# Splitting step 11 of sixteen rounds as well, with the cast of that step on ScalarE

## The chip, the cores and the metric

The kernel runs on one core of one Trainium2 chip. The metric is the device time of one execution in microseconds, as the median of repeated runs; less is better. The chip's engines have short names in what follows: PE is TensorE (matmuls), PEld its weight loads, DVE is VectorE, ACT is ScalarE, POOL is GpSimd, SP is SyncE, which issues the DMAs. Each engine works through its own instructions in the order in which they were written, and waits on semaphores for those of other engines.

## The reference, cut to what matters

The program computes an agent attention over two batches of 12480 tokens with 128 channels and 49 agents, and then a two-layer network with an ELU between the layers:

```python
a2k = sm(agents, k); agent_v = a2k @ v          # softmax over the 12480 keys
q2a = sm(q, agents); x = q2a @ agent_v          # softmax over the 49 agents
h = x @ w_in                                    # 128 -> 2048
g = np.where(h > 0.0, h, np.exp(np.minimum(h, 0.0)) - 1.0)
out = g @ w_out                                 # 2048 -> 128
```

All of it is in float32.

## The kernel before

The tokens are cut into 26 groups of 960, called rounds (13 per batch). The product `agent_v @ w_in` is folded into one small matrix per batch, so that a round needs only the 49 softmax weights of each token. A round has 16 steps: two halves of 480 token columns on each of two row groups, times eight chunks `c` of 256 hidden units. Step `s` is round `s // 16`, and its number in the round is `s % 16`; chunk `c` is `s % 8`. Step 11 of a round is thus chunk 3 of the second half.

One step is a chain across engines:

- `p1(s)` (L406): six matmuls (L413) make `h` for 256 hidden units and 960 tokens in a PSUM buffer of two banks. There are three such buffers, taken in turn by `slot()` (L151). The same three serve the attention work.
- `elu(s)` (L415): ACT computes `e = relu(-h)` (L419) and `e = exp(-e)` (L422), DVE computes `g = max(e - 1, h)` (L424), after which the PSUM buffer is free.
- `split(s)` (L426): in the steps for which `is_split(s)` holds, DVE rounds `g` to `hi` in the format float32r (L431), and POOL computes the remainders `lo = g - hi` as two instructions (L204, a helper). There are three buffers for `hi` and three for each `lo`.
- `p2(s)` (L436), which runs four steps later (`LAG = 4`) behind `p1(s + 4)`: the second layer (L453), added up in PSUM over the eight chunks. Where the step is split it is 12 matmuls in float32r: `w_lo * hi`, `w_hi * hi` and `w_hi * lo`, over two halves of the chunk and two row groups. Where it is not split it is 4 matmuls in float32, each of which the trace shows as two.

`SPLITS` lists the chunks that are split: 1, 3, 4, 6, 7 in general, and 1, 4, 6, 7 in the second half of a round that is "covered". A round is covered when there is a visit at its step 11. A visit (L629) is a piece of attention work that takes one of the three PSUM buffers at the end of a step: scores of later queries (`q`), scores of the second batch's keys (`k`), or products with its values (`e`). Visits at step 11 are in rounds 0 to 10 and in rounds 12, 14, 16, 18, 20 and 22; in rounds 1 to 8 there is another one at step 1. In steps 4 and 12 that are not covered, `p1` of the next step is issued one step early.

The order on each engine is written out by hand: the loop at the end (L722 on) issues, for each step, `p1`, `p2` of four steps earlier, `elu`, `split`, and then the attention work planned for that step. To a visit at step 11 belong an exponential of 392 columns on ACT (`q_exp`, L307) behind `split` of step 12, reductions on DVE at steps 12 to 14, and in rounds 4 to 7 also subtractions on DVE (`e_sub`, L208) and exponentials on ACT (`e_exp`, L211) at steps 13 and 14. In the last step of each half the partial sums leave PSUM: ACT copies `oa` (L468) between the two activations of steps 3 and 11, and POOL adds (L469).

The lines that decide what is split:

```python
SPLITS = ((1, 3, 4, 6, 7), (1, 4, 6, 7))                                   # L49
return c in SPLITS[half if j * NM + NP + LAG in covered else 0]            # L403
```

Of the kernel before, what the change touches and what calls it, by code (L numbers as in the profile page):

```python
# [13 lines left out]
ALU = mybir.AluOpType  # L14
# [10 lines left out]
def tile_agent_attention_moe(  # L25
# [10 lines left out]
    nc = tc.nc  # L36
# [5 lines left out]
    NM = DFF // 128  # L42
# [5 lines left out]
    LAG = 4  # L48
    WARM = 2  # L49
    LEAD = 6  # L50
    NP = NM // 2
    EDGE = (NP - 1 + LAG) % NP
    SPLITS = ((1, 3, 4, 6, 7), (1, 4, 6, 7))
# [143 lines left out]
    def cast_hi(eng, out, x):  # L197
        if eng is nc.scalar:
            nc.scalar.activation(out=out, in_=x, func=ACTF.Copy)
        else:  # L200
            eng.tensor_scalar(out=out, in0=x, scalar1=1.0, scalar2=0.0, op0=ALU.mult, op1=ALU.add)

    def rest(eng, out, x, hi):
        eng.tensor_tensor(out=out, in0=x, in1=hi.bitcast(F32), op=ALU.subtract)  # L204
# [179 lines left out]
    def wo_hi(c):  # L384
        for x in (2 * c, 2 * c + 1):
            if x in SPLIT:
                cast_hi(nc.scalar, w_part(w_hi, x), w_e[x])
# [6 lines left out]
    h_t, e_t, g_t, hi_t, lo_t, o_t = {}, {}, {}, {}, {}, {}  # L394

    def at_step(s):

        x, c = divmod(s, NP)
        return x // 2, x % 2, c

    def is_split(s):
        j, half, c = at_step(s)
        return c in SPLITS[half if j * NM + NP + LAG in covered else 0]  # L403

    def p1(s):
        j, half, c = at_step(s)  # L406
        h = slot()
        ah, al = A[j // NG, c]
        hi, lo = p_t[j]
        for i, (a, p) in enumerate([(ah, hi), (ah, lo), (al, hi)]):  # L410
            for u, r in enumerate(ROWS):
                x = slice(r, r + NA)
                nc.tensor.matmul(out=h[:, u, 0:T], lhsT=a[x, :], rhs=p[u ^ half][x, :], start=i == 0, stop=i == 2)  # L413
        h_t[s] = h[:, :, 0:T]

    def elu(s, between=None):

        h, e = h_t.pop(s), x_p.tile([128, 2, T], F32, tag="e", name="e")
        nc.scalar.activation(out=e, in_=h, func=ACTF.Relu, scale=-1.0)  # L419
        if between:  # L420
            between()
        nc.scalar.activation(out=e, in_=e, func=ACTF.Exp, scale=-1.0)  # L422
        g = g_p.tile([128, 2, T], F32, tag="g", name="g", bufs=5)
        nc.vector.scalar_tensor_tensor(out=g, in0=e, scalar=-1.0, in1=h, op0=ALU.add, op1=ALU.max)  # L424
        g_t[s] = g

    def split(s):
        if not is_split(s):
            return
        hi_t[s] = g_p.tile([128, 2, T], F32R, tag="hi", name="hi", bufs=3)  # L430
        nc.vector.tensor_copy(out=hi_t[s], in_=g_t[s])  # L431
        lo_t[s] = []
        for i in range(2):
            lo_t[s].append(g_p.tile([128, T], F32R, tag=f"lo{i}", name=f"lo{i}", bufs=3))
            rest(nc.vector if s == S - 1 else nc.gpsimd, lo_t[s][i], g_t[s][:, i, :], hi_t[s][:, i, :])

    def p2(s):
# [6 lines left out]
        if is_split(s):  # L444
            x, hi, lo = SPLIT.index(c), hi_t.pop(s), lo_t.pop(s)
            jobs = [(w[:, x, i], hi[:, i, :]) for w in (w_lo, w_hi) for i in range(2)]
            jobs += [(w_hi[:, x, i], lo[i]) for i in range(2)]
        else:
            jobs = [(w_f[:, PLAIN.index(c), i], g[:, i, :]) for i in range(2)]
# [28 lines left out]
    def at(s, fn, *a):  # L478
        pre.setdefault(s, []).append((fn, a))

    with tc.manual_schedule():
        with tc.tile_pool(name="pro", bufs=6) as pro:
# [128 lines left out]
            def A_part(c, eng):  # L611
                A_pe(0, 512 * c, 512 * c + 512, banks[c])
                A_out(0, 512 * c, 512 * c + 512, eng)
# [9 lines left out]
        groups[0] = 32  # L623
        mid = {}
        covered = set()
        visits = {}

        def visit(*work):
# [21 lines left out]
        def plan(s, what):  # L650
            work = [(x[0], int(x[1:])) for x in what.split()]
            assert s not in visits
            for x in work:
                visits[x] = s
            if s % NP == EDGE:
                covered.add(s + 1)
            at(s, visit, *work)

        plan(EDGE, "q1 k0")
        plan(11, "q2 k1")  # L660
        for i in range(4):
            plan(NM * i + 17, f"k{3 * i + 2} k{3 * i + 3}")
            plan(NM * i + 27, f"q{i + 3} k{3 * i + 4}" if i < 3 else "q6")
# [28 lines left out]
        for r in range(NR):  # L692
            s0 = visits["e", r]
            x = 75 + NM * (r // 3)
# [25 lines left out]
        for s in range(S + LAG):  # L720
            after = None
            if s < S and s not in h_t and s != NP - LAG - 1:  # L722
                p1(s)
            if s == 0:
                A_part(2, dve)
                A_part(3, dve)
            if s % NP == LAG and s > LEAD and s not in covered and s + 1 < S:
                p1(s + 1)
            if s == 2:
                t = ps_o.tile([128, 512], F32, tag="o1", name="o1")  # L730
                nc.tensor.matmul(out=t[:, 0:T], lhsT=ident, rhs=win_sb[:, 0:T], start=True, stop=True)
            x = s - LAG + (s < LEAD)
            if x >= 0 and s != LEAD:
                after = p2(x)
            if s == NP - LAG - 1:
                p1(s)
            for fn, a in mid.pop(s, []):
                fn(a)
            if s < S:
                elu(s, after)  # L740
                split(s)
            elif after:
                after()
            for fn, a in pre.pop(s, []):
                fn(*a)
# [34 lines left out]
```

## Time and profile before

| | before |
|---|---|
| median of 3 runs | 997.98 us (997.44 to 998.54) |
| the profiled execution | 998.71 us, span of its instructions 995.9 us |
| granted TensorE clock, mean | 0.996 |
| busy share PE / PEld / DVE / ACT / POOL | 98% / 74% / 85% / 89% / 69% |
| steps split, of 416 | 243 |
| length of a round | 33.8 to 38.2 us |

The profiled execution took 998.71 us, of which 995.9 us lie between the first and the last instruction on record; the other 2.8 us stand around it. All durations below come from that execution. PE is busy nearly all the time, and so what the other engines do matters only where PE waits for it. A "busy" PE includes matmuls whose modelled ends overlap the start of the next, so the chain of waits, which gives each stretch of time to one piece of work, is the better view for what a group of matmuls costs.

### The profile page before, as it was taken

Reading aid. Unit: us, or ns where it says so; the run is one execution under the profiler, and the core shown is the slowest. Engines: PE = TensorE matmul, PEld = TensorE weight load, DVE = VectorE, ACT = ScalarE, POOL = GpSimd, SP = SyncE. Lnnn points to the kernel's source line nnn. Section 1 sums busy time; section 2 is a strip of 40 time slices with the busy share of each in tenths; the row PEclk is TensorE's granted clock in tenths of the full one; section 3 lists DMA queues with packets and bytes.
Section 4 is the critical chain, followed back from the end, with each engine's and each line's share of the span. In section 5 each row is a group of like instructions: output and inputs, shape, how many; then the busy total and the mean of one; then the engine's idle time right before and its main releaser. Section 6 shows DMA issues by size and latency. Waiting matters only on the chain.

```text
span 995.9 us, 25483 instructions
## 1 busy us (share of the span) xinstructions
PE 978.3 (98%) x10380; PEld 734.3 (74%) x10380; DVE 849.7 (85%) x1028; ACT 884.3 (89%) x1017; POOL 687.0 (69%) x559
## 2 busy tenths in 40 slices
PE   7899999999999999999999999999999999999998
PEld 5767777777777777877777777777777777777775
DVE  7778888888888878888888898898888888988887
ACT  4588998988988889998998999989999989989996
POOL 3146666666666766766786886877868867867886
PEclk8999999999999999999999999999999999999999
DMA  9942222223232211101101101011020021001000
GB/s 349 385 148 89 80 72 81 78 74 96 68 85 66 66 41 46 38 31 65 36 23 55 37 26 62 26 56 41 18 76 27 21 66 37 26 12 37 27 20 21
DMA packets 25983, 67.30 MB, mean 68 GB/s; under 512 B 3083, under 2 KB 14963, under 8 KB 25867
## 3 DMA queue, kind: packets, MB, share of 16 engines
q1 hardware_dynamic: 25867, 65.69, 19.5%
q8 instruction: 81, 1.33, 0.6%
q14 instruction: 35, 0.29, 0.1%
HBM read 43.11 MB, written 12.78 MB: 56 GB/s over the span
## 4 chain that ended last, share of the span: by engine, by line
PE 93%; DVE 2%; ACT 2%; DMA 2%; issue 1%; POOL 0%; SPq 0%; DVEq 0%; ACTq 0%
PE o L453 59%; PE h L413 27%; PE h L291 2%; PE h L219 2%; PE h L160 1%; DMA v<-in_vx_dram 1%; PE h L331 1%; DVE g L424 1%; DMA k<-in_kT_dram 1%; ACT e L419 1%; ACT e L422 0%; PE o L160 0%; DVE m_all L168 0%; DVE ex L107 0%; ACT ex L103 0%
## 5 line engine op out<-in xcount | busy, mean ns | idle before, releaser
L204 POOL TENSOR_TENSOR lo<-g,hi 128x480 fp32r<-128x480 f32 x484 | 603.3, 1272 | 253.6 <-DVE hi L431 190.3
L424 DVE SCALAR_TENSOR_TENSOR g<-e,h 128x960 f32<-128x960 f32 x416 | 478.2, 1150 | 109.2 <-ACT e L422 91.7
L419 ACT ACTIVATE e<-h 128x960 f32<-128x960 f32 x416 | 402.5, 967 | 41.0 <-PE h L413 38.5
L422 ACT ACTIVATE e<-e 128x960 f32<-128x960 f32 x416 | 419.1, 1007 | 11.6
L453 PE MATMUL o<-g,w_f 64*128 64x480 f32 x1384 | 307.8, 562 | 0.2 <-DVE g L424 0.2
L413 PE MATMUL h<-py,ahi 49*128 49x480 f32 x832 | 292.4, 431 | 1.4 <-DVE g L424 0.7
L413 PE MATMUL h<-px,ahi 49*128 49x480 f32 x832 | 292.4, 431 | 0.1
L431 DVE CAST hi<-g 128x960 fp32r<-128x960 f32 x243 | 198.4, 816 | 10.8
L453 PEld LDWEIGHTS o<-g,w_f 64*128 64x128 f32 x1384 | 133.2, 185 | 83.1 <-issue 73.6
L413 PEld LDWEIGHTS h<-py,ahi 49*128 49x128 f32 x832 | 149.9, 186 | 39.3 <-issue 23.4
L413 PEld LDWEIGHTS h<-px,ahi 49*128 49x128 f32 x832 | 149.9, 186 | 26.3 <-issue 17.0
L453 PE MATMUL o<-hi,w_lo 64*128 64x480 f32 x972 | 159.4, 403 | 0.0
L413 PE MATMUL h<-px,alo 49*128 49x480 f32 x416 | 157.0, 377 | 0.0
L413 PE MATMUL h<-py,alo 49*128 49x480 f32 x416 | 157.0, 377 | 0.0
L453 PE MATMUL o<-lo,w_hi 64*128 64x480 f32 x972 | 146.9, 378 | 0.0
L453 PE MATMUL o<-hi,w_hi 64*128 64x480 f32 x972 | 146.0, 376 | 0.0
L453 PEld LDWEIGHTS o<-hi,w_lo 64*128 64x128 f32 x972 | 93.4, 186 | 26.0 <-issue 14.3
L453 PEld LDWEIGHTS o<-lo,w_hi 64*128 64x128 f32 x972 | 92.6, 184 | 13.6 <-POOL lo L204 0.3
L453 PEld LDWEIGHTS o<-hi,w_hi 64*128 64x128 f32 x972 | 92.5, 184 | 13.0
L413 PEld LDWEIGHTS h<-py,alo 49*128 49x128 f32 x416 | 76.6, 184 | 5.7
L413 PEld LDWEIGHTS h<-px,alo 49*128 49x128 f32 x416 | 76.6, 184 | 5.6 <-DVE alo L275 0.2
L469 POOL TENSOR_TENSOR ob<-ob,oa 128x480 f32<-128x480 f32 x51 | 70.0, 1372 | 12.2 <-ACT oa L468 12.2
(89 smaller groups left out, 517.7 us busy)
## 6 DMA issues: line engine op xcount, KB each, us to landing
k<-in_kT_dram SPq DMA_DIRECT2D x26, 480.0 KB
q<-in_qT_dram SPq DMA_DIRECT2D x26, 480.0 KB
out_dram<-ob SPq DMA_DIRECT2D x51, 240.0 KB
py<-px SPq DMA_DIRECT2D x104, 91.9 KB
v<-in_vx_dram SPq DMA_DIRECT2D x13, 516.0 KB
v<-in_vx_dram SPq DMA_DIRECT2D x13, 483.8 KB
raw<-in_w_in_dram SPq DMA_DIRECT2D x4, 512.0 KB
raw<-in_w_out_dram SPq DMA_DIRECT2D x4, 512.0 KB
```

The source lines that it names most:

```text
L160: nc.tensor.matmul(out=ps[u:u + w, j * NA:(j + 1) * NA], lhsT=src[:, x:x + w], rhs=ag_sb[:, b, :], start=True, stop=True)
L204: eng.tensor_tensor(out=out, in0=x, in1=hi.bitcast(F32), op=ALU.subtract)
L219: nc.tensor.matmul(out=ps[u:u + 64], lhsT=e[:, j * NA:j * NA + 64], rhs=v_t[b, r][:, j, :], start=(r == rs[0] and j < 2), stop=(r == rs[-1 ...
L291: nc.tensor.matmul(out=ps[u:u + w, t * NA:(t + 1) * NA], lhsT=src[:, x:x + w], rhs=ag_sb[:, j // NG, :], start=True, stop=True)
L331: nc.tensor.transpose(ps[:NA2, u, i * HP:(i + 1) * HP], pp[x, i, 0:NA2], ident[x, x])
L413: nc.tensor.matmul(out=h[:, u, 0:T], lhsT=a[x, :], rhs=p[u ^ half][x, :], start=i == 0, stop=i == 2)
L419: nc.scalar.activation(out=e, in_=h, func=ACTF.Relu, scale=-1.0)
L422: nc.scalar.activation(out=e, in_=e, func=ACTF.Exp, scale=-1.0)
L424: nc.vector.scalar_tensor_tensor(out=g, in0=e, scalar=-1.0, in1=h, op0=ALU.add, op1=ALU.max)
L431: nc.vector.tensor_copy(out=hi_t[s], in_=g_t[s])
L453: nc.tensor.matmul(out=o_t[u][:, 0:T], lhsT=w[x], rhs=v[x, :], start=first and i == 0, stop=last and i == len(jobs) - 1)
L469: nc.gpsimd.tensor_tensor(out=ob, in0=ob, in1=oa, op=ALU.add)
```

## The change

In the sixteen covered rounds after round 0, step 11 is split too, so that in those rounds the second half has the same split chunks as the first. The cast of that step goes to ACT instead of DVE, and it is issued one step later: behind the exponential of step 12, ahead of the cast and remainders of step 12. Round 0 stays as it was. The helper `cast_hi` now issues a plain copy where it is called for an engine other than ACT; before, all its calls were for ACT, and `split` issued the plain copy itself.

```diff
-            eng.tensor_scalar(out=out, in0=x, scalar1=1.0, scalar2=0.0, op0=ALU.mult, op1=ALU.add)
+            eng.tensor_copy(out=out, in_=x)
 ...
-        return c in SPLITS[half if j * NM + NP + LAG in covered else 0]
+        return c in SPLITS[half if j == 0 else 0] or by_act(s)
+
+    def by_act(s):
+        x = s - s % NM
+        return 0 < x and (s % NM == NP + EDGE and x + NP + EDGE in steps_of_visits)
 ...
         hi_t[s] = g_p.tile([128, 2, T], F32R, tag="hi", name="hi", bufs=3)
-        nc.vector.tensor_copy(out=hi_t[s], in_=g_t[s])
+        cast_hi(nc.scalar if by_act(s) else nc.vector, hi_t[s], g_t[s])
 ...
             if s < S:
                 elu(s, after)
-                split(s)
+                if s and by_act(s - 1):
+                    split(s - 1)
+                if not by_act(s):
+                    split(s)
```

How the instructions move is the same in each of the sixteen rounds; round 12 stands for them (its step 11 is step 203 of 416). The line numbers of the changed kernel are 4 higher from `elu` on, and its buffers have other numbers. On PE, `p2` of step 11 stands behind `p1` of step 15. Before, it reads `g_7354`, the output of step 11's ELU, with the plain weights `w_f`:

```order
L413 MATMUL h_7509<-py0_6766,alo_776 128x480
L413 MATMUL h_7509<-px0_6765,alo_776 128x480
L453 MATMUL o0_7436<-g_7354,w_f_88 128x480
L453 MATMUL o1_7437<-g_7354,w_f_88 128x480
L453 MATMUL o0_7436<-g_7354,w_f_88 128x480
L453 MATMUL o1_7437<-g_7354,w_f_88 128x480
L413 MATMUL h_7531<-px0_7216,ahi_6296 128x480
```

At the same place of the changed kernel, between `p1` of step 15 and `p1` of step 16, PE has these rows, which read `hi` and `lo` of step 11:

```order
L457 MATMUL o0_7576<-hi_7587,w_lo_90 128x480
L457 MATMUL o1_7577<-hi_7587,w_lo_90 128x480
L457 MATMUL o0_7576<-hi_7587,w_lo_90 128x480
L457 MATMUL o1_7577<-hi_7587,w_lo_90 128x480
L457 MATMUL o0_7576<-hi_7587,w_hi_89 128x480
L457 MATMUL o1_7577<-hi_7587,w_hi_89 128x480
L457 MATMUL o0_7576<-hi_7587,w_hi_89 128x480
L457 MATMUL o1_7577<-hi_7587,w_hi_89 128x480
L457 MATMUL o0_7576<-lo0_7589,w_hi_89 128x480
L457 MATMUL o1_7577<-lo0_7589,w_hi_89 128x480
L457 MATMUL o0_7576<-lo1_7591,w_hi_89 128x480
L457 MATMUL o1_7577<-lo1_7591,w_hi_89 128x480
```

Four float32 matmuls became twelve in float32r; the other rows of PE keep their order. On ACT, these are the rows of before from the first activation of step 12 to the first of step 15; `qe` is the exponential that belongs to the visit:

```order
L419 ACTIVATE e_7442<-h_7429 128x960
L422 ACTIVATE e_7442<-e_7442 128x960
L307 ACTIVATE qe_7423<-qe_7423 124x392
L419 ACTIVATE e_7477<-h_7458 128x960
L422 ACTIVATE e_7477<-e_7477 128x960
L419 ACTIVATE e_7496<-h_7485 128x960
L422 ACTIVATE e_7496<-e_7496 128x960
L419 ACTIVATE e_7520<-h_7509 128x960
```

The same stretch of ACT in the changed kernel:

```order
L423 ACTIVATE e_7582<-h_7569 128x960
L426 ACTIVATE e_7582<-e_7582 128x960
L199 ACTIVATE hi_7587<-g_7494 128x960
L307 ACTIVATE qe_7563<-qe_7563 124x392
L423 ACTIVATE e_7623<-h_7604 128x960
L426 ACTIVATE e_7623<-e_7623 128x960
L423 ACTIVATE e_7642<-h_7631 128x960
L426 ACTIVATE e_7642<-e_7642 128x960
```

One activation of 128x960 came in, behind step 12's exponential and ahead of `qe`. On POOL, the addition of the output sums of step 11 is followed in before by the remainders of steps 12 and 14:

```order
L469 TENSOR_TENSOR ob_7346<-ob_7346,oa_7345 128x480
L204 TENSOR_TENSOR lo0_7449<-g_7445,hi_7447 128x480
L204 TENSOR_TENSOR lo1_7451<-g_7445,hi_7447 128x480
L204 TENSOR_TENSOR lo0_7503<-g_7499,hi_7501 128x480
L204 TENSOR_TENSOR lo1_7505<-g_7499,hi_7501 128x480
```

And in the changed kernel by those of steps 11, 12 and 14:

```order
L473 TENSOR_TENSOR ob_7486<-ob_7486,oa_7485 128x480
L204 TENSOR_TENSOR lo0_7589<-g_7494,hi_7587 128x480
L204 TENSOR_TENSOR lo1_7591<-g_7494,hi_7587 128x480
L204 TENSOR_TENSOR lo0_7595<-g_7585,hi_7593 128x480
L204 TENSOR_TENSOR lo1_7597<-g_7585,hi_7593 128x480
L204 TENSOR_TENSOR lo0_7649<-g_7645,hi_7647 128x480
L204 TENSOR_TENSOR lo1_7651<-g_7645,hi_7647 128x480
```

Two remainders came in ahead of those of step 12. DVE and SP keep their rows and their order. Over the whole program there are 16 activations, 32 subtractions on POOL and 128 matmul rows more.

## Rows read from the trace of the kernel before

**Rows 1.** Page: busy time and share of each engine; chain that ended last, by engine.

```profile
PE 978.3 (98%) x10380; PEld 734.3 (74%) x10380; DVE 849.7 (85%) x1028; ACT 884.3 (89%) x1017; POOL 687.0 (69%) x559
...
PE 93%; DVE 2%; ACT 2%; DMA 2%; issue 1%; POOL 0%; SPq 0%; DVEq 0%; ACTq 0%
```

**Rows 2.** Longest wait of PE, whole span: us in total, times, longest us.

```profile
PE h L160 <- DMA k<-in_kT_dram: 4.9, 3, 3.5
```

**Rows 3.** Chain of waits, round 12, from p2 of step 11: start us, us, what.

```profile
536.71 1.61 PE o L453 x8
538.32 0.65 PE h L413 x6
538.97 1.31 PE o L453 x12
540.28 0.66 PE h L413 x6
```

**Rows 4.** Chain of waits, round 13, the same; no visit, step 11 split.

```profile
570.59 1.30 PE o L453 x12
571.89 0.65 PE h L413 x6
572.54 1.31 PE o L453 x12
573.85 0.65 PE h L413 x6
```

**Rows 5.** Costliest groups: ACT's exponential, whole span; then its cast of w_out.

```profile
L422 ACT ACTIVATE e<-e 128x960 f32<-128x960 f32 x416 | 419.1, 1007 | 11.6
...
L199 ACT ACTIVATE w_hi<-even x4: 417/418/420, 24.8 to 51.3; 128x256 fp32r<-128x256 f32 x4
```

**Rows 6.** Timeline of ACT, round 12 from step 12, then round 13: [idle before <-releaser].

```profile
531.22 1.01 ACT L422 ACTIVATE e<-e 128x960 f32<-128x960 f32 x1
532.13 0.52 ACT L307 ACTIVATE qe<-qe 124x392 f32<-124x392 f32 x1
532.56 0.95 ACT L419 ACTIVATE e<-h 128x960 f32<-128x960 f32 x1
...
545.20 0.98 ACT L419 ACTIVATE e<-h 128x960 f32<-128x960 f32 x1
546.49 0.57 ACT L468 ACTIVATE oa<-o 128x480 f32<-128x480 f32 x1 [0.32 <-PE o L453]
...
547.86 0.97 ACT L419 ACTIVATE e<-h 128x960 f32<-128x960 f32 x1
548.85 1.01 ACT L422 ACTIVATE e<-e 128x960 f32<-128x960 f32 x1
549.77 0.96 ACT L419 ACTIVATE e<-h 128x960 f32<-128x960 f32 x1
```

**Rows 7.** Timeline of POOL, round 12, remainders of step 12, then 14 and 15.

```profile
534.64 2.39 POOL L204 TENSOR_TENSOR lo<-g,hi 128x480 fp32r<-128x480 f32 x2 [4.50 <-DVE hi L431]
538.98 5.18 POOL L204 TENSOR_TENSOR lo<-g,hi 128x480 fp32r<-128x480 f32 x4 [1.95 <-PE h L413]
```

**Rows 8.** Timeline of PE, round 12: the matmuls of step 12 that read lo.

```profile
539.68 0.60 PE L453 MATMUL o<-lo,w_hi 64*128 64x480 f32 x4
```

**Rows 9.** Timelines, round 5 into 6: ACT, then DVE, then PE.

```profile
278.31 0.53 ACT L211 ACTIVATE s_all<-s_all 120x392 f32<-120x392 f32 x1 [0.34 <-DVE s_all L208]
...
282.02 1.33 DVE L431 CAST hi<-g 128x960 fp32r<-128x960 f32 x1
283.27 1.14 DVE L424 SCALAR_TENSOR_TENSOR g<-e,h 128x960 f32<-128x960 f32 x1
...
285.47 0.48 PE L413 MATMUL h<-px,ahi 49*128 49x480 f32 x1
```

**Rows 10.** DVE's casts and e_sub by line: ns min/median/max, first and last start.

```profile
L431 DVE CAST hi<-g x243: 659/708/1564, 60.3 to 988.1; 128x960 fp32r<-128x960 f32 x122
...
L208 DVE TENSOR_TENSOR s_all<-s_all,mb x26: 514/562/1134, 36.9 to 392.2; 120x392 f32<-120x392 f32 x26
```

More of the change, by code (lines that the diff above doesn't have):

```diff
@@ L625, in tile_agent_attention_moe @@
         covered = set()
+        steps_of_visits = set()
         visits = {}
@@ L654, in plan @@
                 visits[x] = s
+            steps_of_visits.add(s)
             if s % NP == EDGE:
```

## The prediction

> **What bounds the kernel now.** I read the shares of busy time first: PE 98%, ACT 89%, DVE 85%, and 93% of the chain that ended last is PE [rows 1]. A high share alone does not make PE the limit, so PE's waits come next: the longest in total is 4.9 us, for keys loaded in the prologue [rows 2]. In the rounds PE is the limit, and PE time saved there is time saved, as long as ACT, DVE and POOL keep up. PE has no slack, ACT little; the reader should look at both around step 11.
>
> The chain of waits then prices the piece that changes. In round 12, which has a visit, the second layer of step 11 takes 1.61 us of the chain and that of step 12, which is split, 1.31 us [rows 3]. In round 13, which has none, step 11 is split already and takes 1.30 us [rows 4]: the state that the change brings, seen on the same chip.
>
> **The change part by part.** *The matmuls.* From the start of step 11's second layer to the first matmul of step 17 are 540.28 - 536.71 = 3.57 us in round 12 [rows 3] and 573.85 - 570.59 = 3.26 us in round 13 [rows 4]. The difference, 0.31 us, includes what a float32 group does to the matmuls behind it; the two entries alone give 1.61 - 1.30 = 0.31 as well. Sixteen rounds change (1 to 10, and the even ones from 12 to 22), so 16 x 0.31 = 5.0 us leave PE.
>
> *The cast on ACT.* Before has no ACT cast of this size. From below: the same operation on 256 columns takes 0.418 us. From above: that row scaled by 960/256 gives 1.57 us, if nothing in it were fixed. The nearest row in shape is the exponential, 128x960 in SBUF, at 1.007 us [rows 5], and in a full queue the next instruction starts 0.91 us after it (531.22 to 532.13) [rows 6]. I take 0.91. Behind the cast in ACT's queue stand the visit's exponential and the activations of step 13 on; DVE waits for those to make `g`, and PE for the PSUM buffer that `g` frees, three allocations later.
>
> Who hides it? Back to back, two activations take 549.77 - 547.86 = 1.91 us a step. In round 12 the first activations of steps 13 and 19 are 545.20 - 532.56 = 12.64 us apart; six steps need 11.46, so ACT has 1.18 us to spare. PE arrives 0.31 us earlier from step 16 on, which leaves 0.87. The cast overruns this by 0.04. Then `oa` of step 19 starts 546.49 - 545.20 = 1.29 us after the activation ahead of it, where back to back it would be 0.99 (547.86 to 548.85), and waits for PE [rows 6]: 0.30 more. So ACT is level with PE again in step 19, before the tight place of steps 20 and 21, where `p1` runs one step ahead. The rounds built like this one (8, 9, 10 and the six from 12 on) keep their 0.31 us each. Rounds 1 to 3 have a visit at step 1 of the next round, in which PE is busy with other work; they keep it too. If the cover is gone, each 0.1 us by which the cast exceeds 0.91 + 0.26 = 1.17 costs 9 x 0.1 us.
>
> *Rounds 4 to 7.* Here ACT has two more exponentials behind the visit, and the second waits 0.34 us for a subtraction on DVE [rows 9], which itself stands behind `g` of step 13 and so moves with the cast. ACT carries most of the 0.91 us into the next round. What that reaches: `g` of step 0 runs on DVE from 283.27 to 284.41, and `p1` of step 2 takes its PSUM buffer at 285.47 [rows 9]; the margin is 1.06 us, or 0.75 with PE 0.31 us early. A full shift of 0.91 makes PE wait 0.16 us there. None of it arrives if DVE's own delay before that `g` (the cast of step 15 took 1.33 us there against 0.66 undisturbed) takes part of the shift; 0.16 + 0.57 = 0.73 if one subtraction also takes its longest time, 1.134 us, in place of 0.562 [rows 10]. Between 0 and 0.73 I take 0.2, near the plain shift: 4 x 0.2 = 0.8 us.
>
> *The remainders on POOL.* Two more a round, 2.39 us a pair [rows 7]. With `hi` of step 11 done near 532.13 + 1.0 = 533.1, its pair ends near 535.6 and the pair of step 12 near 538.1, a microsecond later than before. PE starts step 11's second layer at 536.71 [rows 3] and reads `lo` in its last third; it reads step 12's `lo` at 539.68 [rows 8], 0.31 earlier after the change, which leaves 539.37 - 538.1 = 1.3 us. POOL's next pair started at 538.98 [rows 7], so POOL has caught up by then. Cost 0, at most 0.2 us a round if a pair took 1.5 us longer.
>
> *The rest.* Buffers of `hi` are reused three casts later: that of step 11 by step 15, cast after PE has passed the second layer of step 11. The other form of the helper is reached only from `split`, where it issues the copy that DVE ran before. Both cost 0; a late buffer would show as a wait of DVE's cast.
>
> *A rule against the change.* DVE's cast of `hi` takes 0.659 to 1.564 us and the subtraction 0.514 to 1.134 for one shape [rows 10]. The Trainium skill, page "SBUF — State Buffer", section "Who interferes with whom", says that VectorE and GpSimd share one pair of ports as an exclusive lock, held for a whole instruction, against casts and against operations with two inputs in SBUF, while ScalarE waits for nobody. The trace's spread agrees with it. By that rule the changed kernel puts DVE's cast of step 12 and the subtractions of steps 13 and 14 beside a POOL that now works some 5 us on end, and the upper bounds would hold in rounds 4 to 7; without it the lower ones would. The sum above goes by the rows.
>
> *The sum.* 5.0 - 0.8 = 4.2 us. The profiled execution took 998.71 us (span 995.9 and 2.8 around it), so it would take 994.5. It stood 0.73 above the median of the three runs, 997.98; against that median the forecast is 997.98 - 4.2 = 993.8 us, 0.42% less.
>
> **The rivals.**
>
> 1. *DVE behind POOL takes most of it.* With the upper bound in rounds 4 to 7, 4 x 0.73 = 2.9 us, the gain is 2.1 us: 995.9. For it speaks the spread of the casts; against it, that DVE is late there only if POOL holds on in just those moments, and that PE's next visit gives 2 us in which to catch up.
>
> 2. *The cast is long and ACT becomes the limit* (the slower side). At 1.57 us ACT's queue would be 1.57 - 0.09 - 0.91 = 0.57 us later than in my sum. Nine rounds then stall 0.57 - 0.26 = 0.31 us each, 2.8 us; rounds 4 to 7 stall 0.73 + 0.57 = 1.3 us each, 5.2 us. Together 8.0 against 5.0: 3.0 us slower, 1001.0. The sign turns at a cast of about 1.34 us: with 0.34 in place of 0.57, nine rounds lose 0.7 us and four lose 4.3. Against it: activations of this width take 0.95 to 1.01 us and one of half the width 0.57 [rows 6], so that a fixed part is there and the scaled bound is too high.
>
> 3. *The split does not pay behind the visit.* If `lo` of step 11 or 12 came late, PE would wait for POOL what the matmuls save: 998.0. The margins of 1.3 us and more speak against it.
>
> **How the numbers follow.** A change within 0.2%, 2 us, is about what a measurement of this kernel cannot tell from none. The forecast has 0.82 (own range 993.0 to 995.0: all of 5.0 kept, or twice the loss taken), rival 1 has 0.10, rival 2 has 0.04, rival 3 has 0.04. Faster than 996.0 is nearly all of the forecast and half of rival 1: 0.84. Within 0.2%: 0.11. Slower: 0.05. The range goes from 992.4 (5.0 us and half a microsecond of scatter, as the runs of before show) to 996.6, past rival 1.
>
> **What would show each step.** In the changed profile the chain should give 1.30 to 1.32 us for step 11's second layer in all rounds but round 0, with 12 matmuls in place of 8; 16 casts of about 1.0 us on ACT; `oa` of step 19 still waiting for PE in round 12; POOL busy about 39 us more in all; rounds 12, 14 and so on 0.31 us shorter, and rounds 4 to 7 by about 0.1. The forecast is wrong if ACT's `oa` no longer waits for PE there, if PE gains a wait for DVE's `g`, or if PEld waits for POOL's `lo`.

## The result, and the profile after

The changed kernel takes 1007.80 us (median of 4 runs, 1007.44 to 1008.16), the kernel before 997.75 us beside it (997.44 to 998.54): ratio 1.0099, 95% interval 1.0082 to 1.0117. It is 10 us slower; the forecast was 993.8 us, outside of its range of 992.4 to 996.6 and of the other sign. The profiled execution took 1008.16 us, with a span of 1006.3 us against 995.9.

The page of the changed kernel, against [rows 1]:

```profile
PE 979.9 (97%) x10444; PEld 743.1 (74%) x10444; DVE 879.7 (87%) x1028; ACT 894.9 (89%) x1033; POOL 732.7 (73%) x591
...
PE 76%; DVE 9%; ACT 9%; issue 3%; DMA 1%; POOL 1%; SPq 1%; DVEq 0%; ACTq 0%; POOLq 0%
```

PE's share of the chain fell from 93% to 76%, and DVE and ACT stand in it with 9% each. DVE has the same 1028 instructions as before and is busy 30 us longer. That is the first thing to see: instructions that were not touched became longer. By DVE's groups the casts grew by 21 us, an addition on 8 columns by 10 and the product `pp` by 5 (neighbours overlap a little, so the groups add up to more than the busy time).

PE's waits, against [rows 2]; PEld's waits for `g` come to another 18.4 us. Before, the two kinds of waits for `g` came to 0.7 and 2.9 us:

```profile
PE h L160 <- DMA k<-in_kT_dram: 7.3, 4, 3.8
PE h L417 <- DVE g L428: 7.2, 22, 0.7
```

The chain of waits in rounds 12 and 13, where [rows 3] and [rows 4] showed PE alone (start us, us, what):

```profile
541.51 0.66 PE h L417 x6
542.17 1.32 PE o L457 x12
543.49 0.65 PE h L417 x6
544.14 1.30 PE o L457 x12
...
550.31 1.10 PE o L457 x10
551.41 0.03 issue
551.44 1.14 DVE g L428
552.58 0.57 DVE ob L469
553.15 0.01 DVE pp L325
553.16 1.26 issue
554.43 1.15 DVE g L428
...
555.66 0.98 ACT e L423
...
557.58 0.96 ACT e L423
```

At 542.17 stands step 11's second layer: 1.32 us and 12 matmuls where [rows 3] had 1.61 and 8. The saving is there. Eight microseconds later, in steps 2 to 7 of the next round, the chain leaves PE for DVE and ACT. In round 9 the chain shows the way in one piece, from the cast over DVE's addition `z` to `g` of step 14 and from there to ACT's first activation of step 16; in the next round it goes through a pair of POOL's remainders as well:

```profile
427.76 0.90 ACT hi L199
428.66 0.42 ACT qe L307
...
431.07 1.16 DVE g L428
432.22 0.48 DVE z L311
432.71 0.02 issue
432.73 1.19 DVE z L316
...
434.29 1.16 DVE g L428
...
435.53 0.99 ACT e L423
...
446.94 2.81 POOL lo L204 x2
```

The timeline of DVE in round 12 shows the same addition (start us, us, engine, line, [idle before <-releaser]):

```profile
541.00 1.16 DVE L428 SCALAR_TENSOR_TENSOR g<-e,h 128x960 f32<-128x960 f32 x1 [0.57 <-ACT e L426]
542.07 0.56 DVE L311 TENSOR_REDUCE z<-qe 124x8 f32<-124x392 f32 x1
542.66 1.22 DVE L316 SCALAR_TENSOR_TENSOR z<-z 124x8 f32<-124x8 f32 x1
543.81 1.14 DVE L428 SCALAR_TENSOR_TENSOR g<-e,h 128x960 f32<-128x960 f32 x1
...
550.18 1.34 DVE L201 CAST hi<-g 128x960 fp32r<-128x960 f32 x1
...
553.07 1.44 DVE L325 TENSOR_TENSOR pp<-qe,z 124x392 f32<-124x392 f32 x1
554.43 1.14 DVE L428 SCALAR_TENSOR_TENSOR g<-e,h 128x960 f32<-128x960 f32 x1
```

And that of POOL in the same stretch, against [rows 7]:

```profile
538.67 5.18 POOL L204 TENSOR_TENSOR lo<-g,hi 128x480 fp32r<-128x480 f32 x4 [3.07 <-ACT hi L199]
545.81 5.19 POOL L204 TENSOR_TENSOR lo<-g,hi 128x480 fp32r<-128x480 f32 x4 [1.95 <-DVE z L319]
```

POOL works on four remainders in a row, to 543.85. Inside of that stretch DVE starts an instruction on 8 columns, the addition of 1e-9 to the softmax sums, at 542.66, and ends it at 543.88, with POOL's last remainder. ACT has the input of `g` of step 14 ready at 541.80 + 1.01 = 542.81 (below); `g` starts only at 543.81. ACT then waits, since `e` has two buffers and the first activation of step 16 overwrites the one that `g` of step 14 reads. ACT's timeline:

```profile
537.61 0.99 ACT L199 ACTIVATE hi<-g 128x960 fp32r<-128x960 f32 x1
538.50 0.52 ACT L307 ACTIVATE qe<-qe 124x392 f32<-124x392 f32 x1
...
541.80 1.01 ACT L426 ACTIVATE e<-e 128x960 f32<-128x960 f32 x1
...
545.04 0.98 ACT L423 ACTIVATE e<-h 128x960 f32<-128x960 f32 x1 [0.33 <-DVE g L428]
...
551.64 0.57 ACT L472 ACTIVATE oa<-o 128x480 f32<-128x480 f32 x1
```

`oa` of step 19 no longer waits for PE, as it did in [rows 6]: ACT is behind when it comes to the tight steps 20 and 21.

Where the time went, by the length of a round (start of its first matmul to that of the next; change against the profiled execution of before):

| rounds | before, us | changed kernel | matmuls alone (x3) | addition moved (x10) |
|---|---|---|---|---|
| 2 to 4, mean | 37.5 | -0.23 | -0.32 | -0.29 |
| 5 to 8, mean | 38.2 | +0.69 | -0.34 | -0.25 |
| 9, 10, 11 | 36.7, 37.1, 35.3 | +1.49, +0.30, +0.86 | -0.32, -0.33, -0.36 | +0.21, -0.36, +0.24 |
| 13, 15, ... 23, mean | 33.9 | +0.67 | -0.37 | +0.05 |
| 12, 14, ... 22, mean | 35.5 | +0.06 | +0.07 | +0.08 |

The saving falls into the round after the covered one. A round begins at `p1` of its step 0, right behind step 11's second layer, and that start hardly moves: in PE's timeline of round 12 it comes 1.24 us after the first float32 matmul before (536.54 to 537.78), and 1.32 us after the first float32r matmul in the changed kernel (542.01 to 543.33).

### The profile page after: what moved, and what is told of

It is laid out like the page before. It is cut to its first block, busy times and chain, and to the rows that moved or that the text cites. A ratio compares the mean times of both kernels' runs of the same rounds, so it can differ in the third digit from the quotient of the medians.

```text
span 1006.3 us, 25707 instructions
## 1 busy us (share of the span) xinstructions
PE 979.9 (97%) x10444; PEld 743.1 (74%) x10444; DVE 879.7 (87%) x1028; ACT 894.9 (89%) x1033; POOL 732.7 (73%) x591
## 4 chain that ended last, share of the span: by engine, by line
PE 76%; DVE 9%; ACT 9%; issue 3%; DMA 1%; POOL 1%; SPq 1%; DVEq 0%; ACTq 0%; POOLq 0%
PE o L457 48%; PE h L417 24%; DVE g L428 5%; ACT e L423 3%; ACT e L426 3%; PE h L291 2%; DMA k<-in_kT_dram 1%; PE h L160 1%; DVE s_all L208 1%; ACT s_all L211 1%; POOL lo L204 1%; DVE hi L201 1%; ACT hi L199 1%; PE h L331 1%; PE h L219 1%
## 5 line engine op out<-in xcount | busy, mean ns | idle before, releaser
L204 POOL TENSOR_TENSOR lo<-g,hi 128x480 fp32r<-128x480 f32 x516 | 649.0, 1285 | 224.3 <-DVE hi L201 99.6
L457 PE MATMUL o<-g,w_f 64*128 64x480 f32 x1256 | 279.8, 562 | 0.2 <-DVE g L428 0.2
L201 DVE CAST hi<-g 128x960 fp32r<-128x960 f32 x243 | 219.0, 901 | 11.9
L457 PEld LDWEIGHTS o<-g,w_f 64*128 64x128 f32 x1256 | 121.4, 185 | 74.9 <-issue 66.5
L457 PE MATMUL o<-hi,w_lo 64*128 64x480 f32 x1036 | 169.7, 402 | 0.0
L457 PE MATMUL o<-lo,w_hi 64*128 64x480 f32 x1036 | 157.4, 378 | 0.0
L457 PE MATMUL o<-hi,w_hi 64*128 64x480 f32 x1036 | 156.2, 376 | 0.0
L457 PEld LDWEIGHTS o<-hi,w_lo 64*128 64x128 f32 x1036 | 100.1, 186 | 26.4 <-issue 14.3
L457 PEld LDWEIGHTS o<-lo,w_hi 64*128 64x128 f32 x1036 | 99.5, 184 | 14.4 <-POOL lo L204 0.5
L457 PEld LDWEIGHTS o<-hi,w_hi 64*128 64x128 f32 x1036 | 99.4, 184 | 13.4
```

The lines of the kernel that those rows point to most:

```text
L201: eng.tensor_copy(out=out, in_=x)
L457: nc.tensor.matmul(out=o_t[u][:, 0:T], lhsT=w[x], rhs=v[x, :], start=first and i == 0, stop=last and i == len(jobs) - 1)
```

## The experiments

Fourteen kernels ran. Each diff is against the changed kernel unless it says otherwise; ratios are to the kernel before on the same chip. The expectations weigh these theories: A, the loss comes from ACT's queue, which the cast shifts; P, it comes from POOL's remainders, which hold DVE off; L, the sharper form of P, a DVE instruction with two inputs in SBUF is held until POOL's current work ends; W, the amount of DVE's work counts and not the hold; M, the saving of the matmuls is not there.

**x1: the cast alone.**

```diff
+        if by_act(s):
+            hi_t.pop(s)
+            return
...
-        if is_split(s):
+        if is_split(s) and not by_act(s):
```

> The changed kernel with the cast of step 11 on ScalarE alone: no remainders on GpSimd and the plain matmuls as before (the cast's output is not used). Theory P (the loss comes from GpSimd's four remainders in a row, which hold VectorE off): about as before, 998 us, at most 999, with VectorE's casts at their old mean of 816 ns. Theory A (the loss comes from ScalarE's queue, shifted by 0.9 us in sixteen rounds): most of the 15 us between forecast without losses (993) and result (1007.8) stays, less what PE's earlier arrival adds, so 1002 to 1008.

Measured 999.44 us, ratio 1.0012 (1.0003 to 1.0022). DVE's casts kept 821 ns (816 in before). The cast by itself costs about 1 us in all. This speaks for P, and against A as the whole cause. Two things are easier here than in the changed kernel: PE keeps the plain matmuls, so it does not come 0.31 us earlier, and the cast shifts the addition past POOL's one pair, so that it takes 196 ns in the mean.

**x2: the cast cut to 8 columns.**

```diff
+        if by_act(s):
+            hi_t[s] = hi_t[s - 2]
...
+            if by_act(s) and i == 0:
+                cast_hi(nc.scalar, lo_t[s][0][:, 0:8], g_t[s][:, 0, 0:8])
```

> The changed kernel with ScalarE's cast cut from 960 columns to 8, so that ScalarE's queue is hardly shifted while GpSimd does the same remainders behind the same place of ScalarE and PE the same matmuls (they read hi of step 9 in place of hi of step 11). Theory P: still slower than before, 1002 to 1008 us, with VectorE's casts near 900 ns. Theory A: near 993 to 994 us. If both are needed together, in between and below 998.

Measured 998.99 us, ratio 1.0012 (1.0002 to 1.0021): between the two. GpSimd's work takes back the 4.8 us of the matmuls and 1 more, but not the 14.6 us that the full change loses. Neither theory alone holds; the cast (1 us) and the remainders (6 us over x3) together cost twice their sum. The addition is held here nearly as long as in the changed kernel, 779 ns in the mean against 820 (lines at x10), while ACT's `oa` of step 19 waits for PE again, 0.30 us at 546.20: the hold does its full damage only where ACT is late too.

**x3: the matmuls alone.**

```diff
+        if by_act(s):
+            hi_t[s], lo_t[s] = hi_t[s - 2], lo_t[s - 2]
+            return
```

> Step 11's second layer as twelve float32r matmuls in the sixteen rounds, reading hi and lo of step 9; no cast and no remainders of step 11. Both theories: the saving of PE alone, 16 x 0.31 = 5.0 us, so 992.8 us. If the saving itself is not there (theory M: PE's earlier arrival runs into ScalarE and VectorE at once), 996 to 998.

Measured 993.20 us, ratio 0.9954 (0.9939 to 0.9969): 4.8 us faster than before. The term of the forecast for the matmuls was right.

**x4: without the small addition.**

```diff
-        if half == 0:
-            nc.vector.scalar_tensor_tensor(out=z, in0=z, scalar=1e-9, in1=z, op0=ALU.add, op1=ALU.max)
-        else:
+        if half:
```

> The changed kernel without the addition of 1e-9 to the softmax sums (a VectorE instruction on 124x8 values with both inputs in SBUF, 1.22 us in step 13 of round 12 against 0.39 undisturbed; the sums are at least 1). Theory P: this instruction is one of those held off, so that g of step 14 comes up to 0.8 us earlier in sixteen rounds; part of the loss goes, 1000 to 1005 us. Theory A: ScalarE's shift stays, 1006 to 1008.

Measured 997.49 us, ratio 0.9994 (0.9984 to 1.0004), 10 us below the changed kernel, more than P expected. 26 instructions on 8 columns decide over the whole loss against the kernel before, and over 10 of the 14.6 us against x3. The 0.39 us that the expectation calls undisturbed was already a hold: in round 5 of before the addition ends at 277.41 + 0.39 = 277.80 with POOL's pair, 275.39 + 2.38 = 277.77; free of POOL it takes 0.16 (x10).

**x6: the same without the change (control).** The edit of x4 on the kernel before.

> Control: the kernel before without the same small addition. Theory L: there GpSimd works on one pair at that place and the addition took 0.39 to 0.75 us off the path of PE, so 997 to 998 us, no change to speak of. If the addition costs by itself, as work, it would gain here too: 988 to 994 us.

Measured 997.91 us, ratio 0.9991 (0.9982 to 1.0001): nothing that can be told from no change. The addition costs only where the change put it.

**x8: another instruction in its place.**

```diff
-            nc.vector.scalar_tensor_tensor(out=z, in0=z, scalar=1e-9, in1=z, op0=ALU.add, op1=ALU.max)
+            nc.vector.tensor_reduce(out=z, in_=q_st[j]["e"], axis=AX.X, op=ALU.add)
```

> The changed kernel with the small addition to the softmax sums replaced by a repetition of the reduction ahead of it: 0.55 us of VectorE with one input in SBUF, in the same place of its queue, in place of an instruction of 8 columns with two inputs in SBUF. Theory L (that instruction is held until GpSimd's pair ends): near the time without it, 997 to 999 us. Theory W (it is VectorE's amount of work that counts, and any instruction there delays g of step 14): 1005 to 1009 us, since the repetition is longer than the 0.39 us that the addition takes undisturbed.

Measured 1004.00 us, ratio 1.0052 (1.0037 to 1.0067). Between the two again: rounds 13 to 23 lose 0.07 us instead of 0.67, as L has it, but rounds 5 to 8 still lose 0.63. That looks like W, but the trace shows a hold there too: the reduction is not held (561 ns in the mean of 26), and the subtraction behind it, which has two inputs in SBUF, is. From DVE and POOL, round 5:

```profile
278.54 0.56 DVE L316 TENSOR_REDUCE z<-qe 124x8 f32<-124x392 f32 x1
279.02 1.17 DVE L208 TENSOR_TENSOR s_all<-s_all,mb 120x392 f32<-120x392 f32 x1
...
274.56 5.21 POOL L204 TENSOR_TENSOR lo<-g,hi 128x480 fp32r<-128x480 f32 x4 [2.90 <-ACT hi L199]
```

POOL's four remainders end at 279.77. Five of these subtractions take 1.15 to 1.17 us here, where the changed kernel has 0.55 or 0.56. So the hold moved on by one instruction, and W has no run that speaks for it alone.

**x10: the addition one step later.** All work is kept.

```diff
-            at(s0 + 2, q_rz, j, 0)
-            at(s0 + 3, q_rz, j, 1)
+            at(s0 + (2 if j == 1 else 3), q_rz, j, 0)
+            at(s0 + (3 if j == 1 else 4), q_rz, j, 1)
```

> The changed kernel with the same small addition one step later (behind the cast of step 14, where GpSimd waits for that cast and holds nothing) and the reciprocal behind it one step later too. Nothing is left out. Theory L (GpSimd's lock on that instruction carries the larger part): 997 to 1000 us, as without the instruction, and its mean time falls from 820 ns to near 200. Theory W (the amount of VectorE's work carries it): 1004 to 1008 us.

Measured 997.65 us, ratio 0.9996 (0.9987 to 1.0005). L's time. The instruction's mean by DVE's groups: in the kernel before

```profile
L316 DVE SCALAR_TENSOR_TENSOR z<-z 124x8 f32<-124x8 f32 x26 | 10.8, 417 | 0.9
```

in the changed kernel

```profile
L316 DVE SCALAR_TENSOR_TENSOR z<-z 124x8 f32<-124x8 f32 x26 | 21.3, 820 | 0.9
```

and moved by one step (x10):

```profile
L316 DVE SCALAR_TENSOR_TENSOR z<-z 124x8 f32<-124x8 f32 x26 | 4.5, 173 | 0.1
```

and in x2, in its old place with a cast of 8 columns on ACT:

```profile
L316 DVE SCALAR_TENSOR_TENSOR z<-z 124x8 f32<-124x8 f32 x26 | 20.3, 779 | 0.9
```

The same work takes 173, 417, 779 or 820 ns in the mean, by what POOL does beside it. Here its place in x10, between two pairs of remainders:

```profile
537.36 0.66 DVE L201 CAST hi<-g 128x960 fp32r<-128x960 f32 x1
537.94 0.16 DVE L316 SCALAR_TENSOR_TENSOR z<-z 124x8 f32<-124x8 f32 x1
538.12 1.15 DVE L428 SCALAR_TENSOR_TENSOR g<-e,h 128x960 f32<-128x960 f32 x1
539.38 1.72 DVE L201 CAST hi<-g 128x960 fp32r<-128x960 f32 x1
```

The cast of step 15 behind it still takes 1.72 us, beside a pair of POOL's.

**x5 and x7: three buffers for `e`**, with the addition in its place and without it.

```diff
-    x_p = ctx.enter_context(tc.tile_pool(name="x", bufs=2))
+    x_p = ctx.enter_context(tc.tile_pool(name="x", bufs=3))
```

> The changed kernel with three buffers for e in place of two (the scratch pool of the prologue ends with it, to make room). Theory L with the buffer of e as the way back to ScalarE (the first activation of step 16 waited 0.33 us for g of step 14, that of step 5 0.66 us): ScalarE no longer waits, a part of the loss goes, 1000 to 1004 us. If PE's wait is set by g and the PSUM buffers alone: 1006 to 1008 us.

> The changed kernel without the small addition and with three buffers for e. Both theories of the buffer: if e's buffer carries what is left of the loss (4 us over the matmuls alone), 994 to 996 us, faster than before; if not, 997 to 998 us.

Measured 1004.92 us for x5 (ratio 1.0060, 1.0045 to 1.0075) and 996.67 us for x7 (0.9982, 0.9972 to 0.9991). The third buffer gives back some 3 us, most of it in the rounds from 9 on (0.41 instead of 0.67 in the odd ones from 13) and in the last; rounds 5 to 8 stay at 0.68. Of it, 0.4 us lie in rounds 0 and 1, ahead of the first split, and x9 shows them without the change; the rest is what the way back through `e`'s buffer carries. With the addition gone the third buffer brings about 1 us.

**x12 and x13: shorter instructions on POOL.** x12 cuts the remainders of steps 11 and 12, x13 those of six steps behind x10's edit.

```diff
+            n = T // 2 if by_act(s) or s and by_act(s - 1) else T
+            for x in range(0, T, n):
+                rest(nc.vector if s == S - 1 else nc.gpsimd, lo_t[s][i][:, x:x + n], g_t[s][:, i, x:x + n], hi_t[s][:, i, x:x + n])
```

> The changed kernel with GpSimd's remainders of steps 11 and 12 cut into instructions of 240 columns in place of 480 (twice as many, by estimate 0.69 us each in place of 1.22, from the 0.724 us of 256 columns). Theory L: VectorE is held until GpSimd's current instruction ends, which is now half as long, so its waits shrink although GpSimd works longer in all: 1001 to 1005 us. If GpSimd's total time counts and not the length of one instruction: 1008 to 1012 us.

> The changed kernel with the small addition one step later, and GpSimd's remainders of steps 11, 12, 14 and 15 and of steps 1 and 3 of the next round cut into instructions of 240 columns. Nothing is left out. Theory L (the 4.5 us that stay over the matmuls alone are VectorE's casts and products behind GpSimd's instructions: the cast of step 15 took 1.72 us there): shorter holds give back some, 994 to 996.5 us. Theory A (they are ScalarE's shift by its cast): 997 to 999 us.

Measured 1002.04 us for x12 (ratio 1.0037, 1.0023 to 1.0050): 6 us off the loss with POOL busy longer, as L has it. The addition fell from 820 to 362 ns in the mean. Rounds 5 to 8 still lose 0.51 us, since the subtraction is held there as in x8 (five times 1.13 or 1.14 us). But 1002.66 us for x13 (1.0045, 1.0032 to 1.0059), 5 us above x10: a miss of both theories. POOL in x13, round 13:

```profile
533.52 5.78 POOL L204 TENSOR_TENSOR lo<-g,hi 128x240 fp32r<-128x240 f32 x8 [3.06 <-ACT hi L199]
539.99 9.12 POOL L204 TENSOR_TENSOR lo<-g,hi 128x240 fp32r<-128x240 f32 x12 [0.69 <-DVE z L316]
```

POOL has 6% more to do (687.4 us for its remainders, against 647.8 in x10) and works 9 us on end, on the remainders of steps 14 and 15 of round 12 and of step 1 of round 13. This time PE itself waits for them: PEld's waits for `lo` come to 3.7 us in 9 times, against 0.3 us once in x10. Here is the wait for step 15's `lo`, and `oa` behind it:

```profile
546.22 0.19 PEld L460 LDWEIGHTS o<-lo,w_hi 64*128 64x128 f32 x2 [0.39 <-POOL lo L204]
546.74 0.57 ACT L475 ACTIVATE oa<-o 128x480 f32<-128x480 f32 x1 [0.57 <-PE o L460]
```

From `oa` on the chain of the round goes through ACT, up to PE's next wait at 553.98. That is the mechanism of rival 3, at step 15 instead of 11 or 12. DVE's casts are held there too, 1.32 us at 549.50 and 1.68 at 555.29, and how the loss divides between the two was not measured.

Shorter holds help where one of them lies on the path, but not when POOL's total grows until PE waits for its output.

**x14: the addition later, and the cast cut to 8 columns.** The edits of x10 and x2 together.

> The changed kernel with the small addition one step later and ScalarE's cast cut to 8 columns (the matmuls of step 11 read hi of step 9). Theory A: ScalarE's shift is gone and with it the rest of the loss, 993 to 994.5 us. Theory L: GpSimd's holds stay, 996 to 998 us.

Measured 994.16 us, ratio 0.9960 (0.9947 to 0.9972): A's time for the rest. DVE's cast of step 15 still took 1.67 us and the product `pp` 1.04 us; they no longer matter once ACT is not late. The four corners, in us:

| | full cast on ACT | cast of 8 columns |
|---|---|---|
| addition in its place | 1007.8 | 999.0 |
| addition one step later | 997.65 | 994.16 |

The hold on the addition alone costs 4.8 us (999.0 against 994.16), the full cast alone 3.5 us (997.65 against 994.16), and the two together 13.6 us, 5.3 more than their sum. The kernel before on the chips of these four runs differs by 0.6 us at most (997.75 to 998.34).

**x9 and x11: a version that beats both, and its control.** x9 is the kernel before without the addition and with three buffers for `e`; x11 has these too, and splits step 11 in eight of the rounds.

```diff
-        return 0 < x and (s % NM
+        return 0 < x and x // NM in (1, 2, 3, 4, 5, 6, 7, 9) and (s % NM
-        return c in SPLITS[half if j == 0 else 0] or by_act(s)
+        return c in SPLITS[half if j * NM + NP + LAG in covered else 0] or by_act(s)
```

> Control for the next: the kernel before without the small addition and with three buffers for e. It waits little for either (the addition alone changed nothing that could be measured): 996.5 to 998.5 us.

> A version meant to be faster than both: without the small addition, with three buffers for e, and step 11 split (cast on ScalarE) in rounds 1 to 7 and 9 alone, where the run with both edits showed the following round 0.26 to 0.37 us shorter; in rounds 8, 10 and the even ones from 12 on it showed nothing or a loss. 8 x 0.31 = 2.5 us less than the control: 994.5 to 996 us. If the step 11 split pays nowhere once ScalarE and VectorE are counted, as the control.

Measured 997.81 us for x9 (ratio 0.9995, 0.9986 to 1.0004) and 995.55 us for x11 (0.9976, 0.9966 to 0.9985). The split pays 2.3 us in these eight rounds, which were chosen by x7, where the round behind each of them was shorter; why the others have no room was not tested by itself. x11 is faster than the kernel before by 0.24% and than the changed one by 1.2%.

## Why the prediction was wrong, point by point

- **The matmuls: right.** 5.0 us forecast, 4.8 us measured by x3, and 1.32 us in the chain.
- **The cast's own size: right.** 0.99 us each, 0.89 us to the next start (537.61 to 538.50), where I took 1.0 and 0.91. Rival 2, a long cast, fell.
- **PE waiting for the remainders: right at nothing.** PEld's waits for `lo` are 0.5 us in all (0.3 in before). Rival 3 fell as it was put. POOL's own end was not quite without a price, though: in rounds 10 and 11 the chain goes through a pair of remainders of step 3 (2.81 us at 446.94), for which DVE's `g` of step 6 waits; before, no round had POOL on the chain. POOL was also busy 46 us more instead of 39.
- **"ACT is level with PE again in step 19": the step that failed.** It treated ACT's 1.18 us between steps 13 and 19 as free for the cast, as if ACT waited for PE alone, and shifted DVE's and POOL's work along with it as if each kept its length; with it fell the "cost 0" of the remainders, which looked at their own end and not at what they hold. The cast put `g` of step 13 nearly 1 us later; POOL's remainders of step 11, which ended nowhere on PE's path, filled the very stretch into which DVE's next instruction was shifted; it took 1.22 us there, against 0.75 in round 12 of before and 0.16 free; and ACT, with two buffers for `e`, had to wait for the `g` behind it. The two effects that I priced one by one (0.04 and 0) cost 14.6 us together against x3: x1 shows 1 us for the cast without the rest, x2 6 us for the remainders with hardly any cast, x10 10 us back for moving one instruction. Two of the three signs of being wrong came: `oa` of step 19 no longer waits, and PE and PEld wait for `g`; PEld did not come to wait for `lo`.
- **Rounds 4 to 7: the place right, the size wrong.** Forecast a loss of 0.2 us each, at most 0.73; measured 1.0 (from -0.34 in x3 to +0.69). The same chain as above, with the subtractions behind the addition. x4 and x10 take it away almost whole (-0.32 and -0.25).
- **Rounds 8 to 10 and 12 to 22: the cover that was not there.** Forecast no loss; measured 1.0 us in each of the rounds 13, 15 to 23, and 0.6 to 1.8 in 9 to 11. Moving the addition (x10) gives rounds 13 to 23 back only 0.6 us each; the rest goes with the cast (x14: -0.37 in rounds 13 to 23, as in x3). Rounds 1 to 3 kept most of their saving, as forecast: -0.23 in rounds 2 to 4 against -0.32 in x3.
- **Rival 1 had the mechanism, with 0.10 and the wrong bounds.** It kept the holds to rounds 4 to 7 and to casts and subtractions [rows 10]. The instruction that decided was not in my rows at all. In before it took 0.75 us in round 12 and 417 ns in the mean, for 8 columns; where POOL does nothing beside it (x10) it takes 0.16 us, 173 ns in the mean of all 26. That was to be seen, and I passed over it as small. In the changed kernel it ends at 542.66 + 1.22 = 543.88, with POOL's 538.67 + 5.18 = 543.85. A hold lasts for one of POOL's instructions, not for all four: with the instructions cut in half (x12) the addition takes 0.45 to 0.52 us in fifteen of the sixteen rounds, against 1.19 to 1.23, and in round 12 it ends there at 540.39 + 0.50 = 540.89, while POOL's row of eight goes on to 536.41 + 5.79 = 542.20. The rule that I weighed, from the Trainium skill, page "SBUF — State Buffer", section "Who interferes with whom", covers it, since the instruction reads `z` twice and so has two inputs in SBUF; the trace agrees with the rule here.

What stays open: x14 (994.16 us) and x3 (993.20) ran on different chips, and their ratios, 0.9960 and 0.9954, cannot be told apart, so it is not shown that the remainders still cost anything there. No run has the full cast and the shorter matmuls without the remainders; how much of the cast's 3.5 us needs POOL beside it is not known. Nor was the third kind of hold, on the product `pp` (870 ns in before, 1066 after), tried by itself.

## What to carry to other kernels

When work is given to an idle engine, ask not only when it ends but what it holds while it runs: here POOL's 2.4 us a round cost little by their own end and most of 10 us through DVE's waits beside them. Idle time that two edits use must be counted once: a shift of 1 us on one engine cost 3.5 us by itself, a hold of 1 us on another 4.8, and the two together 13.6. Look in the groups for short instructions whose mean is far above their size; one of them, moved by one step in the order, was worth 10 us. Whether such a hold lies on the path is another question: in the kernel before, taking the same instruction out was worth nothing that could be measured (x6).

## What the runs showed of the hardware that I had not expected

A VectorE instruction on 8 columns with two inputs in SBUF took between 0.15 us (x13) and 1.25 us (x5), by GpSimd's work beside it. A reduction in the same place, longer but with one input in SBUF, kept its 0.56 us, and the next instruction with two inputs in SBUF took the hold: the subtraction went from 0.55 to 1.17 us (x8). The hold followed the length of one GpSimd instruction: some 1.2 us beside subtractions of 480 columns, 0.45 to 0.52 beside subtractions of 240 (x12). Cutting GpSimd's subtraction of 480 columns in two raised two pairs from 5.18 us to 5.78 (x13): the shorter hold is paid for with total time, which in x13 cost more than it gave.
